# Splitting the segment recurrence into memory rows and other rows, and loading half the heads in the weight gradients, in a training-step kernel on one core

## The chip, the cores and the metric

One NeuronCore of a Trainium2 chip runs the whole program. The metric is device time in microseconds (us) of one execution. A run is "fast" when it lies within 1.5% of the fastest run of the same kernel. The kernel before takes 6604.74 us (median of 4 runs, 6594.03 to 6612.77).

The names used below: PE is the matmul engine, PEld its weight loads, DVE the vector engine, ACT the scalar engine, POOL the third elementwise engine, SP the engine that only issues transfers. PEclk is the share of PE's clock that was granted.

## The reference

The kernel computes the output and all gradients of a recurrent attention layer, gated by a feed-forward layer. What matters here is the attention:

```python
# S = 2048, Dm = 640, H = 32 heads of 128, M = 8 memory rows, segments of 32 rows
for s in range(64):
    h = concatenate([mem, x[32 * s : 32 * s + 32]])        # 40 rows
    q, k, v = h @ Wq, h @ Wk, h @ Wv                       # 32 heads each
    p = softmax(mask(q @ k.T * scale))                     # memory rows see all 40, the others causally
    o = (p @ v) @ Wo                                       # 40 rows of 640
    mem = o[:8]                                            # carried to the next segment
    outs.append(o[8:])                                     # not carried
# ... feed-forward, gate; then the backward pass through the same 64 segments,
#     and the gradients of Wq, Wk, Wv, Wo from the stored q, k, v, o
```

Only eight of the forty output rows are carried from one segment to the next. The other 32 are stored and used later.

## The kernel before

The forward recurrence treats the 40 rows as one block. Each segment builds v, then for three groups of heads (12, 12, 8) the projections, the scores, the softmax and the product with v, and at last the output projection `pso`. The next segment starts from the copy of `pso` into `hT`.

```python
for t in range(T):                                  # T = 64
    hT = hTs[t % 2]
    ...                                             # pv: values of the 8 memory rows, 40 matmuls of 512 columns
    def scores_softmax_group(h0, nh):
        for hh in range(nh):                        # psc: 40x40 scores, one matmul for each head
            nc.tensor.matmul(psc[:, hh, :], qT[:, hidx, :], kT[:, hidx, :], ...)
        nc.vector.tensor_tensor(smv, pscv, k.maskq[0:L, 0:nh, :], ALU.add)
        nc.vector.reduce_max(mx[:, 0:nh], smv, axis=AX.X)
        nc.vector.tensor_tensor(smv, smv, bc_last(mx[:, 0:nh], L), ALU.subtract)
        nc.scalar.activation(exv, smv, ACT.Exp, scale=k.scale)
        nc.vector.tensor_reduce(zs[:, 0:nh], exv, axis=AX.X, op=ALU.add)
        nc.vector.reciprocal(rz[:, 0:nh], zs[:, 0:nh])
        nc.gpsimd.tensor_tensor(Pseg[:, h0:h0 + nh, :], exv, bc_last(rz[:, 0:nh], L), ALU.mult)
    ...                                             # pt_ot_group: ppt, po and their copies to PTseg, oT
    for gi2, (h0, nh) in enumerate(hgroups):
        f1_group(h0, nh)                            # pj: projections, 320 matmuls of 40 columns in all
        scores_softmax_group(h0, nh)
        if gi2 >= 1:
            pt_ot_group(*hgroups[gi2 - 1])
    vt_all()
    pt_ot_group(*hgroups[ng - 1])
    for dc in range(DC):                            # pso: 160 matmuls of 40 columns
        for jc in range(H):
            nc.tensor.matmul(pso[:, dc, :], Wo[:, jc, dc * P:(dc + 1) * P], oT[:, jc, :], ...)
    nc.vector.tensor_copy(hTs[(t + 1) % 2][:, :, 0:M], pso[:, :, 0:M])     # the carried rows
    ...                                             # stores of q, k, v, o, p
```

The last stage builds token-major copies of q, k, v and o, 16 heads ("a half") at a time, from 64 stored tiles each:

```python
ft = srp.tile([P, H, L], BF16, name="fullx", tag="fullx", bufs=10)
k.dma(ft[:], XT[t].rearrange("p (h l) -> p h l", l=L))                     # all 32 heads, 320 KB
...
nc.vector.tensor_copy(xsrc[:, :, j, :], fulls[j][:, hs:hs + H2, M:L])      # 16 of them are used
```

One helper issues nearly all transfers.

```python
self.dma_engines = [nc.sync, nc.scalar]
def dma(self, out, in_, eng=None):
    if eng is None:
        eng = self.dma_engines[self._dma_i % len(self.dma_engines)]
        self._dma_i += 1
    return eng.dma_start(out, in_)
```

## Time and profile before

| | before |
|---|---|
| time, median of 4 runs | 6604.74 us |
| span of the profiled run | 6603.7 us |
| forward recurrence (first `pv` to first epilogue transpose) | 1886.5 us |
| backward recurrence (first `pgh` to first `w2acc`) | 2259.4 us |
| weight gradients of the attention (first `gacc` to last `oacc`) | 1098.4 us |

The profile page of the kernel before begins with busy times. It then shows the span in 40 equal slices of 165 us; each digit is a share in tenths (busy share for PE, granted clock for PEclk, busy share of the transfer engines for DMA).

```profile
PE 5397.4 (82%) x112777; PEld 4213.5 (64%) x112978; DVE 2551.8 (39%) x5102; ACT 1765.0 (27%) x3076; POOL 346.0 (5%) x782
...
PE   6868887777777766999999999999555877888878
...
PEclk9888777777777767999899998999757998999989
DMA  5363332222222255222222222222666855455552
```

Slices 4 to 14 are the forward recurrence: PE at 7 or 8, its clock at 7 or 8, transfers at 2 or 3. Nothing is full there. From the 35th slice on, the weight gradients show PE at 7 or 8 with the clock at 8 or 9 and transfers at 4 or 5 until the last slice: short stretches in which loads, not PE, set the pace. These are the two places at which the change aims.

### The profile page before, as it was taken

What the parts mean: (1) busy time and instruction counts of PE and PEld (TensorE: products, weight loads), DVE (VectorE), ACT (ScalarE), POOL (GpSimd) and SP (SyncE); (2) the same over time, 40 slices, a digit from 0 to 9 for tenths busy, and PEclk for the clock granted to TensorE, in tenths of its full rate; (3) what the DMA queues carried; (4) which work ended last, traced back from release to release, by engine and by line L of the source; (5) the groups of instructions that cost most, each with busy time, mean ns of one, the idle gap of its engine ahead of it and who ended that gap; (6) DMA issues with size and microseconds to landing.
All of it is one profiled execution on the core that took longest, in us unless ns stands there. A gap on an engine that the chain in (4) does not pass through costs nothing.

```text
span 6603.7 us, 244712 instructions
## 1 busy us (share of the span) xinstructions
PE 5397.4 (82%) x112777; PEld 4213.5 (64%) x112978; DVE 2551.8 (39%) x5102; ACT 1765.0 (27%) x3076; POOL 346.0 (5%) x782
## 2 busy tenths in 40 slices
PE   6868887777777766999999999999555877888878
PEld 3426777666766656888888888888422444444445
DVE  5424544444444443444434334433225622222222
ACT  3313333223223221222222222222113112232222
POOL 0000000000000000000000000000000001111110
PEclk9888777777777767999899998999757998999989
DMA  5363332222222255222222222222666855455552
GB/s 179 126 218 110 100 112 66 63 67 61 63 67 61 63 152 201 79 78 79 79 73 78 75 76 78 75 76 78 72 191 202 192 138 199 148 185 201 181 169 99
DMA packets 795893, 760.71 MB, mean 115 GB/s; under 512 B 444016, under 2 KB 625264, under 8 KB 790256
## 3 DMA queue, kind: packets, MB, share of 16 engines
q1 hardware_dynamic: 452638, 375.93, 19.5%
q10 hardware_dynamic: 338450, 348.15, 17.1%
q8 instruction: 883, 14.47, 0.9%
q0 software_dynamic: 3776, 20.97, 0.8%
q14 instruction: 146, 1.20, 0.1%
HBM read 453.95 MB, written 290.89 MB: 113 GB/s over the span
## 4 chain that ended last, share of the span: by engine, by line
PE 60%; DMA 15%; DVE 12%; issue 5%; ACT 4%; POOL 2%; ACTq 0%; another core or an unknown queue 0%; POOLq 0%; DVEq 0%; SPq 0%
PE pgh L806 12%; PE gacc L1160 5%; PE pso L579 5%; PE pj L518 4%; PE pgo L729 4%; PE oacc L1186 2%; PE pv L497 2%; POOL Pseg L541 2%; PE pgot L782 2%; PE pgxb L968 2%; DMA hb_tok<-HB 2%; PE ptokk L774 2%; PE pvx L471 2%; DMA fullx<-GQT 2%; PE wacc L1042 2%
## 5 line engine op out<-in xcount | busy, mean ns | idle before, releaser
L1160 PE MATMUL gacc<-gtok_all,h_all 128*128 128x512 bf16 x2322 | 554.3, 387 | 42.2 <-ACT gtok_all L94 10.8
L579 PE MATMUL pso<-oT,Wo 128*128 128x40 bf16 x10240 | 379.3, 197 | 74.0 <-ACT oT L94 73.9
L1160 PEld LDWEIGHTS <-h_all 128*128 128x128 bf16 x2400 | 236.0, 99 | 313.8 <-issue 73.6
L579 PEld LDWEIGHTS <-Wo 128*128 128x128 bf16 x10240 | 355.5, 107 | 45.9 <-issue 34.2
L806 PE MATMUL pgh<-gQT,WqT 128*128 128x40 bf16 x10240 | 348.8, 182 | 11.1 <-issue 7.0
L806 PE MATMUL pgh<-gKT,WkT 128*128 128x40 bf16 x10240 | 330.3, 181 | 22.8 <-DMA WkT<-WKT 14.0
L94 ACT COPY qtok<-ptokq 40x1024 bf16<-40x1024 bf16 x128 | 128.8, 1006 | 768.5 <-PE ptokq L774 759.8
L806 PE MATMUL pgh<-gVT,WvT 128*128 128x40 bf16 x10240 | 320.2, 181 | 10.2 <-issue 9.0
L518 PE MATMUL pj<-hT,Wq 128*128 128x40 bf16 x10240 | 322.3, 185 | 0.2
L806 PEld LDWEIGHTS <-WqT 128*128 128x128 bf16 x10240 | 303.6, 97 | 22.3 <-issue 9.0
L518 PEld LDWEIGHTS <-Wq 128*128 128x128 bf16 x10240 | 296.3, 100 | 33.6 <-issue 28.2
L806 PEld LDWEIGHTS <-WkT 128*128 128x128 bf16 x10240 | 294.0, 97 | 28.3 <-DMA WkT<-WKT 14.1
L518 PE MATMUL pj<-hT,Wk 128*128 128x40 bf16 x10240 | 309.9, 185 | 0.8 <-ACT oT L94 0.6
L811 DVE CAST goT<-pgh 128x40 bf16<-128x40 f32 x63 | 12.6, 199 | 767.0 <-PE pgh L806 767.0
L806 PEld LDWEIGHTS <-WvT 128*128 128x128 bf16 x10240 | 289.6, 96 | 13.9 <-issue 11.5
L729 PE MATMUL pgo<-goT,WoT 128*128 128x40 bf16 x10240 | 277.9, 180 | 25.0 <-DMA WoT<-WOT 15.2
L518 PEld LDWEIGHTS <-Wk 128*128 128x128 bf16 x10240 | 293.4, 100 | 1.1 <-issue 1.0
L729 PEld LDWEIGHTS <-WoT 128*128 128x128 bf16 x10240 | 268.1, 96 | 34.8 <-DMA WoT<-WOT 15.3
L541 POOL TENSOR_TENSOR Pseg<-ex,rz 40x480 bf16<-40x480 bf16 (+1 forms) x192 | 171.9, 895 | 2229.1 <-DVE rz L540 2210.7
L1129 PE MATMUL pt<-ident,xsrc 128*128 128x128 bf16 x2048 | 162.1, 237 | 115.5 <-DVE xsrc L1118 63.0
L1129 PEld LDWEIGHTS <-xsrc 128*128 128x128 bf16 x2048 | 141.5, 107 | 169.0 <-issue 80.8
L1121 POOL COPY msrc<-fullx 128x128 bf16<-128x128 bf16 x512 | 152.8, 324 | 1685.0 <-DMA fullx<-GQT 980.4
(228 smaller groups left out, 9116.8 us busy)
## 6 DMA issues: line engine op xcount, KB each, us to landing
fullx<-GQT SPq DMA_DIRECT2D x64, 320.0 KB
fullx<-GQT ACTq DMA_DIRECT2D x64, 320.0 KB
fullx<-GKT SPq DMA_DIRECT2D x64, 320.0 KB
fullx<-GKT ACTq DMA_DIRECT2D x64, 320.0 KB
fullx<-GVT SPq DMA_DIRECT2D x64, 320.0 KB
fullx<-GVT ACTq DMA_DIRECT2D x64, 320.0 KB
fullx<-OT SPq DMA_DIRECT2D x64, 320.0 KB
fullx<-OT ACTq DMA_DIRECT2D x64, 320.0 KB
```

The lines of the kernel that those rows point to most:

```text
L471: nc.tensor.matmul(pvx[:, :], xnTt[:, dc, :], Wv[:, dc, jn * 512:(jn + 1) * 512], start=(dc == 0), stop=(dc == DC - 1))
L497: nc.tensor.matmul(pv[32 * q:32 * q + M, :], hT[:, dc, 0:M], Wv[:, dc, jn * 512:(jn + 1) * 512], start=(dc == 0), stop=(dc == DC - 1), til ...
L518: nc.tensor.matmul(pj[:, hh, :], W_[:, dc, hidx * P:(hidx + 1) * P], hT[:, dc, :], start=(dc == 0), stop=(dc == DC - 1))
L541: nc.gpsimd.tensor_tensor(Pseg[:, h0:h0 + nh, :], exv, bc_last(rz[:, 0:nh], L), ALU.mult)
L579: nc.tensor.matmul(pso[:, dc, :], Wo[:, jc, dc * P:(dc + 1) * P], oT[:, jc, :], start=(jc == 0), stop=(jc == H - 1))
L729: nc.tensor.matmul(pj[:, hh, :], WoT[:, dc, hidx * P:(hidx + 1) * P], goT[:, dc, :], start=(dc == 0), stop=(dc == DC - 1))
L774: nc.tensor.transpose(ptk[:, hh, :], src[:, b8 + hh, :], k.ident[:, :])
L782: nc.tensor.transpose(ptk[:, hh, :], gOT[:, hs + b8 + hh, :], k.ident[:, :])
L806: nc.tensor.matmul(pso[:, dc, :], WT_[:, jc, dc * P:(dc + 1) * P], gX[:, jc, :], start=(i_acc == 0), stop=(i_acc == n_acc - 1))
L1121: nc.gpsimd.tensor_copy(msrc[:, mt2, :, r4, j * M:(j + 1) * M], fulls[j][:, hs:hs + H2, 0:M])
L1129: nc.tensor.transpose(pt8[0:nrow, hh, :], xsrc[:, b8 + hh, 0:nblk, :], k.ident[:])
L1160: nc.tensor.matmul(accs[dc][:, :], h_all[:, kt, dc * P:(dc + 1) * P], gtok[:, kt, jn * 512:(jn + 1) * 512], start=(kt == 0), stop=(kt == N ...
```

## The change

Its intent is twofold. First, the chain that is carried from segment to segment shall hold only what the eight memory rows need: 8 rows x 32 heads = 256 rows, packed into two blocks of 128. The other 32 rows of segment t are worked on one step later, beside the memory rows of segment t+1. Second, the last stage shall load only the 16 heads it uses, into 24 buffers instead of 10. The core of the diff:

```diff
+        def mem_attention(t, qT, kT, vtile):
+            for hidx in range(H):          # psT: scores of 8 rows, keys on the partitions
+                nc.tensor.matmul(psT[:, hidx, :], kT[:, hidx, :], qT[:, hidx, 0:M], start=True, stop=True)
+            nc.scalar.copy(sTm[:], psT[:])
+            for g in range(NGT):           # two transposes: 256 rows on the partitions
+                nc.tensor.transpose(ps2[:, g, :], sTm2[:, g * P:(g + 1) * P], k.ident[0:L, 0:L])
+            nc.vector.reduce_max(mx[:], ps2[:], axis=AX.X)
+            ...
+                nc.scalar.activation(Em[:, g, :], ps2[:, g, :], ACT.Exp, bias=nmx[:, g:g + 1], scale=k.scale,
+                                     accum_out=Zm[:, g:g + 1])
+            ...                            # rZm, Pm, back by two transposes to PTm
+                nc.tensor.matmul(pom[:, hidx, :], vtile[:, hidx * P:(hidx + 1) * P], PTm2[:, hidx * M:(hidx + 1) * M],
+                                 start=True, stop=True)
+            nc.scalar.copy(oTc[:, :, 0:M], pom[:, :, :])
+        def x_attention(tp, qT, kT, vtile):   # the other 32 rows, as before, of segment t-1
+            ...
-                ex = wk.tile([L, 12, L], BF16, name="ex", tag="ex")
+                ex = wk.tile([NXQ, 12, L], BF16, name="ex", tag="ex")     # the pool had 2 buffers, now 1
+            ...
+        for step in range(T + 1):
+            ...
+                mem_attention(t, qT, kT, vtile)
+            if tp >= 0:
+                x_attention(tp, qTs[tp % 2], kTs[tp % 2], vts[tp % 2])
+            emit_wT_units(units_per_step)     # 3 of the 136 weight transposes
-                    nc.tensor.matmul(pso[:, dc, :], Wo[:, jc, dc * P:(dc + 1) * P], oT[:, jc, :],
+                    nc.tensor.matmul(pso[:, dc, :], Wo[:, jc, dc * P:(dc + 1) * P], oTc[:, jc, :],
@@ backward @@
-            nc.vector.tensor_tensor(prod[:], gOT[:], oT_s[:], ALU.mult)
+            nc.vector.tensor_tensor(prod[:, :, 0:M], gOT[:, :, 0:M], oT_a[:, :, 0:M], ALU.mult)
+            nc.vector.tensor_tensor(prod[:, :, M:L], gOT[:, :, M:L], oT_b[:, :, M:L], ALU.mult)
@@ weight gradients @@
-                ft = srp.tile([P, H, L], BF16, name="fullx", tag="fullx", bufs=10)
-                k.dma(ft[:], XT[t].rearrange("p (h l) -> p h l", l=L))
+                    ft = srp.tile([P, H2, L], BF16, name="fullx", tag="fullx", bufs=24)
+                    k.dma(ft[:], XT[t].rearrange("p (h l) -> p h l", l=L)[:, hs:hs + H2, :])
```

Left out: the second buffers of q, k and v, the mask tables that are now built after the stage before, the shifted store of o (its memory columns go to row t, the others to row t+1), and the load of two such rows in the backward pass and in the last stage.

## The prediction

> **What bounds the kernel now.** I read three things in this order: busy time by stage, the chain of waits inside one forward step, and busy time in slices of the last stage.
>
> The stages are told apart by which tiles are written. The forward recurrence (64 segments, tile pso) runs from 533 to 2416 us, the backward recurrence (pgh) from 2520 to 4716, and the weight gradients of the attention (gacc, oacc) from 5490 to 6604. Busy time in those stretches (us of PE, PEld, DVE, ACT, POOL, then granted PE clock, DMA share, GB/s):
>
> ```profile
> 533.00:892.00 359.00, 303.96 (x8096) 265.20 (x8096) 176.71 (x358) 134.22 (x249) 31.74 (x35) 0.80 0.33 103
> 892.00:2416.00 1524.00, 1191.55 (x34017) 1068.85 (x34016) 694.95 (x1364) 466.61 (x897) 140.19 (x157) 0.76 0.23 68
> ...
> 2520.00:4716.00 2196.00, 2055.11 (x59121) 1904.80 (x59119) 863.77 (x1528) 584.46 (x1020) 13.62 (x63) 0.92 0.27 80
> ...
> 5490.00:6317.00 827.00, 684.52 (x4250) 361.53 (x4326) 202.24 (x460) 219.17 (x300) 122.77 (x410) 0.94 0.54 182
> ```
>
> The backward stage has PE busy 94% at clock 0.92: little to win there. The forward stage has PE busy 78% at clock 0.76, with DVE at 46% and ACT at 31%. No engine is full, so a chain of dependent steps bounds it. One step takes 28.94 us (pv from 1514.05 to 1542.99). Its chain, by time (start, length, what):
>
> ```profile
> 1514.05 2.33 PE pv L497 x40
> 1516.38 3.88 PE pj L518 x149
> 1520.27 0.47 PE psc L526 x12
> 1520.76 0.66 DVE smx L530
> ...
> 1522.81 0.61 ACT ex L536
> 1523.45 0.65 DVE zs L538
> ...
> 1525.05 0.99 POOL Pseg L541
> ...
> 1533.55 0.47 ACT ex L536
> ...
> 1537.94 0.43 ACT oT L94
> 1538.41 4.30 PE pso L579 x136
> 1542.74 0.21 DVE hT L583
> ```
>
> From 1520.76 to 1538.41 the chain walks through the softmaxes of three head groups on DVE, ACT and POOL; PE fills in projections where it can. The output projection pso waits for the last group, and the next segment waits for pso. In the weight gradient stage, half the heads take 134 us (one transpose block starts at 5647.77, the next at 5782.89, the next at 5917.00). The same columns for one such half, first its dense part, then its build part:
>
> ```profile
> 5710.21:5782.89 72.68, 68.17 (x307) 30.44 (x313) 9.02 (x16) 6.12 (x11) 5.18 (x18) 1.00 0.28 92
> 5782.89:5845.67 62.78, 43.61 (x402) 28.19 (x408) 24.03 (x61) 29.72 (x40) 14.05 (x46) 0.92 0.81 271
> ```
>
> In the build part the DMA share is 0.81, and the waits show what for:
>
> ```profile
> L1118 DVE COPY xsrc<-fullx 128x512 bf16<-128x512 bf16 x43 | 12.2, 313 | 31.1 <-DMA fullx<-GKT 31.0
> ```
>
> So the build is paced by loads: 64 tiles of 320 KB per half (20.5 MB), of which only half the heads are used.
>
> **What the Trainium skill says.** "TensorE: Matmul & The Clock Gate", Back-to-back issue gap: below 64 columns a matmul costs a floor of about 25 ns however narrow it is. The trace agrees: 32 pgh matmuls of 40 columns start 0.812 us apart (3504.66 to 3505.47), 25.4 ns each, and 40x40 ones in the backward step cost the same. So halving the columns of a matmul saves nothing, and each added matmul costs 25 ns. The same page, The HAM clock gate: the PE clock falls to half after an idle window. The trace shows granted 0.76 in the forward against 0.92 in the backward stage; 136 pso matmuls after a stall took 4.30 us, 31.5 ns each. "DMA: Bandwidth & Descriptors", Why small descriptors are slow: about 3 cycles per packet, which at 1280 against 2560 bytes would be some 3% (my estimate from its formula). So halving the run length should nearly halve the load time; no row of this trace shows it alone. "Perfetto Trace Analysis", Optimization Strategy: interleaving regimes with different bounds can help, which is what this change does.
>
> **The change, part by part.**
>
> (1) Forward pipelining. Only the 8 memory rows of segment t feed segment t+1. The change computes these 8 rows for all 32 heads by themselves (packed as 256 rows: two transposes, one softmax of 128x80), and does the other 32 rows one step later, as filler. Their three softmaxes leave the loop-carried chain. I worked the new step out along the new kernel's order of instructions.
>
> PE work: pj 320, pso 160, and five sets of 32 (psT, psc, ppt, po, pvt) plus pom 32 = 672 narrow matmuls, plus 4 transposes: 676 x 25.4 ns = 17.2 us. With pv 2.33 us that is 19.6 us (before: 608 x 25.4 ns + 2.33 = 17.8 us).
>
> The chain: end of pj to sTm = drain 0.2 + last kT copy 0.49 + psT 0.35 + sTm 0.4 (256 columns, between 0.33 for 200 and 0.43 for 320 on ACT) + hand-overs = 1.5. sTm to ps3: psc and ps2 ahead 1.0, then on DVE mmx 0.25, mx 0.65, nmx 0.2, smx 0.65 and subtract 0.65 that stand between in its order, rZm 0.2, vT 0.4, Pm 0.25, hand-overs 0.35: 4.4. Em and the small reductions have no row of their own; I take the fixed cost of the 40-column DVE copies (0.2). Then ps3 0.3 + PTm 0.4 + pom 1.0 + oTc 0.4 = 2.1; pso 160 x 25.4 ns + drain + hT = 4.5; one ppt block 0.3; pv + pj = 10.5. Sum 23.3 us, so PE would still stall 3.7 us. I add 0.5 for a clock not fully granted: 23.8.
>
> Weight transposes: before, they ran inside the first steps (tile wTpt, 542 to 892 us), which took 29.4 us instead of 28.9, so they were almost free. Now three units of 4 or 5 transposes stand in each of 46 steps, partly in a stall, partly inside pso; they share one PSUM buffer with pvt, which moves into the pv block. I charge 0.5 + 1.0 = 1.5 us: 25.3 for those.
>
> Forward: 46 x 25.3 + 18 x 23.8 + 9 (a 65th step for the last 32 rows) + 5 (tables now built after the VX stage) = 1606 us, against 1883. Gain 277.
>
> (2) Half loads in the weight gradients. Each load takes the 16 heads in use, 160 KB, and there are 24 buffers instead of 10. Before, 10 tiles and the 16 that sit in four xsrc tiles were ready when a build began: the first 112 transposes ran in 11.7 us. Now 40 of 64 are ready, and the other 24 are 3.9 MB, 14 us at 271 GB/s, behind a build that is bound by PE: 320 transposes x 55 ns + 85 gacc x 216 ns = 36 us, and I allow 42 for short waits on copies (ACT has some 30 us of work there). That replaces 62.8. Five steady halves gain 20 each, the first (5490 to 5648, nothing prefetched) 32, the two of OT 17 and 13, as their PE work is larger: 162, say 165.
>
> (3) Backward: one more 320 KB load per step, hidden (DMA share 0.27), and prod in two pieces, 0.83 us to some 0.9 on DVE, which psD waits for: 64 x 0.1 = 6, say 8 us lost.
>
> Sum: 6605 - 277 - 165 + 8 = 6171, say 6170 us.
>
> **The rivals.** First: the memory chain becomes the new wait. It has a dozen hand-overs between PE, DVE and ACT, each behind other work in a strict order. DVE stands at 13.3 us of 28.9 per step now and gets about 1.5 more, so queueing is likely though the engine isn't full. 2 us more per step would give 6300, still faster. Second: PE becomes the bound and the chain hides in it fully, 21 us per step with the clock at 0.9: 6170 - 64 x 3.5 = 5950. Against it speaks that pso can't start before pom and its copy, and nothing large is left to fill those stalls. Third: the loads of the last stage were hidden anyway, or short runs move no faster per packet, so nothing is gained: 6335. Against it: the 31 us wait of xsrc on fullx per half. Fourth: the build gets as short as PE work alone, 104 us per half: about 60 us better, 6110. A slower kernel would need the forward step to stay above 29 us and the last stage to gain nothing.
>
> **Range and chances.** The forward gain is the uncertain term (200 to 370), the last stage 110 to 220. Taken together 6060 to 6280 should hold it 8 times in 10. Faster by over 2% (below 6473) 0.97, within 2% 0.025, slower 0.005.
>
> **What would show it.** In the changed profile: the distance of hT copies should be near 23.8 late and 25.3 early in the forward stage; the chain there should name psT, sTm, Em, PTm, pom and pso, and no x softmax or POOL; the granted clock there should rise from 0.76 to 0.85 or more. A half of the weight gradients should take some 114 us, with the wait of xsrc on fullx near 5 us instead of 31. The backward step should stay at 34.3 to 34.5 us. I would be wrong if pso waits for x rows (ppt, po), if the stall before ps3 is over 3 us, or if builds still sit at a DMA share of 0.8.

## The result, and the profile after

All outputs are correct. Ratios here are the mean time of one kernel's fast runs over the mean of the other's in the same rounds, so not quite the ratio of the medians.

| | before | after |
|---|---|---|
| time, median | 6602.53 us (12 runs, 6594.03 to 6612.77) | 6266.26 us (8 runs, 6252.06 to 6289.4) |
| ratio, with 95% interval | 1 | 0.949 (0.9477 to 0.9503) |
| span of the profiled run | 6603.7 us | 6287.6 us |

The change gains 336 us of the predicted 434. The profiled run of the kernel after is the slowest of its eight, 23 us above the median, so the stages below sum to 316 us.

The same four lines of the page after the change:

```profile
PE 5450.7 (87%) x117284; PEld 4249.5 (68%) x117490; DVE 2564.7 (41%) x5429; ACT 1816.0 (29%) x3535; POOL 343.6 (5%) x782
...
PE   6859999999998849999999999999745788899989
...
PEclk9878888888888758989899898989855899999999
DMA  5353333333322282222222223222475774433441
```

In the forward slices (5 to 12, of 157 us) PE is now at 9, but its clock is still at 8. From the 35th slice on transfers are down from 4 or 5 to 3 or 4, and PE is at 8 or 9. Stage by stage, from the first instruction of each to that of the next (us):

| stage | before | after | change | predicted |
|---|---|---|---|---|
| up to the forward recurrence | 533.0 | 538.5 | +5.5 | +5 |
| forward recurrence | 1886.5 | 1663.2 | -223.3 | -282 |
| its epilogue | 119.5 | 121.6 | +2.1 | 0 |
| backward recurrence | 2259.4 | 2283.2 | +23.8 | +8 |
| feed-forward gradients, first part (`w2acc`, `pghb`) | 355.2 | 373.9 | +18.7 | 0 |
| feed-forward gradients, second part (`pgxb`) | 348.0 | 353.4 | +5.4 | 0 |
| attention weight gradients | 1098.4 | 949.6 | -148.8 | -165 |

(The prediction's forward gain of 277 includes the 5 us in the first row.)

Below are the stretches of the kernel after: the forward recurrence with weight transposes in its steps, and the later part without them. The columns are the stretch, its length, the busy times of PE, PEld, DVE, ACT and POOL with counts, the granted clock, the share of transfers, and GB/s.

```profile
538.50:1750.00 1211.50, 1150.71 (x34149) 1012.78 (x34150) 652.38 (x1479) 493.58 (x1189) 127.99 (x142) 0.83 0.31 90
1750.00:2197.00 447.00, 403.51 (x12449) 362.78 (x12446) 231.03 (x512) 166.01 (x415) 46.60 (x53) 0.81 0.24 71
```

In the first, PE is busy 95% (1150.71 of 1211.50), in the second 90%. The clock is 0.83 and 0.81, where the prediction asked for 0.85 or more. The distance of successive `hT` copies is 25.7 us in the first 45 intervals (25.3 predicted) and 25.85 in the later ones (23.8 predicted); in the kernel before it was 29.4 on average, 30.6 in the first eleven and 29.2 in the others.

**One early step.** The timeline of PE in the kernel after, with start, length, line, operation, tiles, shape and count:

```profile
1200.51 0.40 PE L617 MATMUL ps<-ident,Pm 128*40 128x128 bf16 x2
...
1201.98 1.01 PE L623 MATMUL pom<-PTm,vt 40*128 40x8 bf16 x32
...
1203.45 5.27 PE L699 MATMUL pso<-oTc,Wo 128*128 128x40 bf16 x160
...
1211.04 1.46 PE L582 MATMUL pv<-Wv,hT 128*8 128x512 bf16 x23
1212.44 1.69 PE L571 MATMUL pj<-hT,Wq 128*128 128x40 bf16 x60
```

The chain is the predicted one: `ps` (the transposes of Pm), `pom`, `pso`, then `pv` and `pj` of the next segment. Matmuls of the other 32 rows (`ppt`, `po`) stand before `pso` in PE's order, but it waits for none of their softmaxes and for no POOL operation: up to 1750 us PE is idle before `pso` in 3 steps only, 1.3 us in all, for the copy of `pom`. But `pso` takes 5.27 us, where 160 matmuls at 25.4 ns were counted as 4.06. The same stretch in slices of one microsecond (columns as above) shows why:

```profile
1196.00:1197.00 1.00, 1.00 (x35) 0.94 (x36) 0.28 (x1) 0.74 (x2) 0.00 (x0) 1.00 0.99 239
1197.00:1198.00 1.00, 1.00 (x36) 0.94 (x33) 1.00 (x3) 0.66 (x2) 0.00 (x0) 0.79 0.41 162
1198.00:1199.00 1.00, 0.98 (x28) 0.91 (x24) 1.00 (x4) 1.00 (x6) 0.00 (x0) 0.50 0.09 18
...
1206.00:1207.00 1.00, 1.00 (x36) 1.00 (x33) 0.00 (x0) 0.29 (x1) 0.68 (x1) 0.50 0.52 164
1207.00:1208.00 1.00, 1.00 (x38) 1.00 (x35) 0.67 (x2) 0.18 (x1) 0.00 (x0) 0.59 0.03 8
1208.00:1209.00 1.00, 1.00 (x41) 0.96 (x37) 0.20 (x1) 0.00 (x0) 0.71 (x1) 1.00 0.05 9
```

The clock falls to 0.50 at about 1197.6, in the stretch of narrow matmuls (`psc`, `po`, `ppt`), and it falls while PE has been busy without a pause (12.6 of the 12.6 us since 1185.0, as far as the profile shows, which models the ends of matmuls). It comes back at 1207.8. Nearly all of `pso` runs at half clock. In the timeline of a later step, 160 `pso` matmuls take 5.49 us, 34 ns each against the 25.4 ns of the prediction; from first start to last end `pso` takes 5.3 us on average in the early steps and 5.2 in the late ones.

"Narrow" needs care here: the projections `pj` have 40 columns too, over the full array, and through them the clock stays at 1.00. What follows them has only 8 columns, or uses only 32 or 40 rows or columns of the array, and some of it is transposes; these three were not told apart. In the early steps the clock fell 1.9 to 5.5 us after the last projection (median 3.7), and 66 of the 67 low stretches of the forward stage last 6.8 or 10.2 us. So a clock that falls before `pso` stays low into it.

**One late step.** The timeline of the kernel after around the end of `pso`, all engines:

```profile
2055.28 5.49 PE L699 MATMUL pso<-oTc,Wo 128*128 128x40 bf16 x160 [0.46 <-ACT oTc L625]
...
2058.17 0.60 ACT L648 ACTIVATE ex<-smx 32x480 bf16<-32x480 f32 x1 [2.45 <-POOL Px L653]
...
2060.92 0.47 ACT L648 ACTIVATE ex<-smx 32x320 bf16<-32x320 f32 x1 [2.15 <-POOL Px L653]
...
2061.42 0.47 DVE L650 TENSOR_REDUCE zs<-ex 32x8 f32<-32x320 bf16 x1 [1.66 <-ACT ex L648]
2061.82 0.18 DVE L703 CAST hT<-pso 128x40 bf16<-128x40 f32 x1
```

`pso` ends at 2060.77. The copy into `hT`, which the next segment needs, starts a microsecond later, because DVE runs in its program order and the sum `zs` of the other 32 rows stands before it. `zs` waits for `ex`, and `ex` waits for POOL to finish with the only buffer of `ex`. The waits of 1800 to 2160 us name it (waiting engine and tile, what it waited for, us in total, times, longest):

```profile
ACT ex L648 <- POOL Px L653: 56.5, 27, 2.5
```

**One half of the weight gradients**, its build part and its dense part, in the kernel after (columns of the stretches):

```profile
5691.08:5733.00 41.92, 39.17 (x405) 26.60 (x411) 24.99 (x66) 31.38 (x43) 11.94 (x41) 1.00 0.64 194
5733.00:5811.30 78.30, 73.50 (x357) 33.88 (x363) 10.48 (x19) 7.37 (x13) 6.31 (x24) 0.98 0.23 72
```

The build part fell from 62.8 to 41.9 us, as predicted (42), with PE busy 93%. The dense part is some 6 us longer than the 72.7 before.

**The feed-forward gradients**, which the change doesn't touch, got slower. First the waits in the kernel before (4798 to 5154 us), then those in the kernel after (4606 to 4980 us), and for each kernel the issues of one load of this stage:

```profile
ACT ghb L937 <- DVE dsl L945: 28.5, 37, 1.1
...
g5t<-GATET SPq DMA_DIRECT2D x52, 128.0 KB
```

```profile
ACT ghb L1062 <- DVE ggT L1074: 66.7, 24, 3.1
...
g5t<-GATET ACTq DMA_DIRECT2D x52, 128.0 KB
```

The load of `g5t` is issued by ACT now and was issued by SP before, although its code is the same: the new forward makes an odd number of calls of the alternating helper. ACT's copy `ghb` now waits for another operation of DVE and for longer.

From this reading came the theory to be tested: the mechanism is as predicted, and what is missing is (a) `pso` at half clock, (b) the `hT` copy behind a softmax that has only one buffer, (c) the swap of the issuing engines. The rivals were that the missing part is PE being simply full, that the depth of the buffers or the bytes were mis-sized in the last stage, or that the two halves of the change disturb each other.

### The profile page after: what moved, and what is told of

The parts are those of the page before. It is cut to its first block, busy times and chain, and to the rows that moved or that the text cites. A ratio compares the mean times of both kernels' runs of the same rounds, so it can differ in the third digit from the quotient of the medians.

```text
span 6287.6 us, 254570 instructions
## 1 busy us (share of the span) xinstructions
PE 5450.7 (87%) x117284; PEld 4249.5 (68%) x117490; DVE 2564.7 (41%) x5429; ACT 1816.0 (29%) x3535; POOL 343.6 (5%) x782
## 4 chain that ended last, share of the span: by engine, by line
PE 67%; DMA 14%; DVE 9%; ACT 5%; issue 3%; POOL 1%; ACTq 0%; another core or an unknown queue 0%; SPq 0%; DVEq 0%; POOLq 0%
PE pgh L931 13%; PE pj L571 8%; PE gacc L1296 6%; PE pgo L853 4%; PE pso L699 3%; PE pv L582 3%; PE oacc L1322 2%; DMA hb_tok<-HB 2%; PE pgxb L1093 2%; PE pgot L907 2%; PE pvx L527 2%; PE ptokk L899 2%; PE ptokq L899 2%; PE wacc L1167 1%; DVE u L873 1%
## 5 line engine op out<-in xcount | busy, mean ns | idle before, releaser
L699 PE MATMUL pso<-oTc,Wo 128*128 128x40 bf16 x10400 | 335.7, 195 | 8.2 <-ACT oTc L625 7.5
L699 PEld LDWEIGHTS <-Wo 128*128 128x128 bf16 x10400 | 335.9, 107 | 9.6 <-issue 6.4
L571 PE MATMUL pj<-hT,Wk 128*128 128x40 bf16 x10240 | 291.6, 180 | 3.2 <-issue 2.6
L571 PEld LDWEIGHTS <-Wq 128*128 128x128 bf16 x10240 | 273.4, 96 | 30.1 <-issue 30.0
L571 PE MATMUL pj<-hT,Wq 128*128 128x40 bf16 x10240 | 290.7, 180 | 1.1 <-ACT qT L94 0.5
L571 PEld LDWEIGHTS <-Wk 128*128 128x128 bf16 x10240 | 274.0, 96 | 4.7 <-issue 4.5
L653 POOL TENSOR_TENSOR Px<-ex,rz 32x480 bf16<-32x480 bf16 (+1 forms) x192 | 173.7, 905 | 1472.8 <-DVE rz L652 678.6
L92 DVE CAST kT<-pj 128x480 bf16<-128x480 f32 (+1 forms) x192 | 115.6, 602 | 301.2 <-PE pj L571 300.8
L92 DVE CAST gwo<-gacc 128x512 bf16<-128x512 f32 x72 | 49.7, 691 | 407.7 <-PE gacc L1296 289.7
L907 PE MATMUL pgot<-ident,gOT 128*40 128x128 bf16 x2048 | 205.5, 256 | 6.1 <-DVE ktok L92 4.5
```

The costliest lines, as they stand in the source:

```text
L92: return nc.vector.tensor_copy(out, in_)
L571: nc.tensor.matmul(pj[:, hh, :], W_[:, dc, hidx * P:(hidx + 1) * P], hT[:, dc, :], start=(dc == 0), stop=(dc == DC - 1))
L653: nc.gpsimd.tensor_tensor(Px[:, h0:h0 + nh, :], exv, bc_last(rz[:, 0:nh], L), ALU.mult)
L907: nc.tensor.transpose(ptk[:, hh, :], gOT[:, hs + b8 + hh, :], k.ident[:, :])
```

## The experiments

Eleven kernels ran, in three groups, each on one chip with runs of the kernel before beside it. All gave correct outputs. Ratios are to the kernel before of the same rounds.

| run | what it is | median us (runs) | ratio (95%) |
|---|---|---|---|
| wg_only | before + half loads | 6431.32 (4) | 0.9724 (0.9699 to 0.9748) |
| fwd_only | after - half loads | 6421.48 (4) | 0.971 (0.9691 to 0.973) |
| ex2 | after + second `ex` buffer | 6251.79 (4) | 0.9456 (0.9432 to 0.948) |
| fillpin | after + useless matmuls on parts of the array | 6461.59 (4) | 0.9768 (0.9748 to 0.9788) |
| parity | after + the old order of issuing engines | 6240.43 (5) | 0.945 (0.9435 to 0.9465) |
| half10 | after with 10 buffers | 6276.3 (4) | 0.9501 (0.9484 to 0.9519) |
| fillfull | after + useless matmuls on the whole array | 6349.19 (4) | 0.9617 (0.9599 to 0.9635) |
| best1 | ex2 and parity together | 6224.34 (4) | 0.9429 (0.9411 to 0.9446) |
| late14 | best1 + 14 useless wide matmuls, late steps only | 6256.11 (4) | 0.9472 (0.9448 to 0.9497) |
| late8 | best1 + 8 of them | 6247.52 (1) | one look |
| latethin | best1 + 94 useless narrow ones | 6287.39 (1) | one look |

### The two parts of the change alone: wg_only and fwd_only

```diff
--- before
+++ wg_only
-  ft = srp.tile([P, H, L], BF16, name="fullx", tag="fullx", bufs=10)
-  k.dma(ft[:], XT[t].rearrange("p (h l) -> p h l", l=L))
+  ft = srp.tile([P, H2, L], BF16, name="fullx", tag="fullx", bufs=24)
+  k.dma(ft[:], XT[t].rearrange("p (h l) -> p h l", l=L)[:, hs:hs + H2, :])
--- after
+++ fwd_only
   the reverse of this, for both loads of the new kernel
```

> Kernel before with part 2 alone (half loads and 24 buffers in the weight gradients). If the parts are independent, as both the prediction and the stage times of the changed kernel say (1098 to 950 us from the first gacc to the last oacc, 149 less), about 6453 us, ratio 0.977. The prediction's own size was 165, which would be 6437 us. Rival: the part only helps together with the new forward stage or the 34 us by which unchanged stages were longer in the changed kernel's profile come from here: then 6490 us or more.

> Changed kernel with the full loads and 10 buffers of before in the weight gradients, so part 1 and part 3 alone. From the stage times of the changed kernel: forward 223 us less, backward 21 us more, start 4 more: about 6402 us, ratio 0.970. If the 21 us of the backward stage are noise of one profile: 6385. The prediction's sizes (277 less, 8 more) would give 6334. The two gains of this and the run before should add up to the whole of 336 us.

wg_only gained 178 us (6609.4 to 6431.32); its weight gradient stage took 928.1 us instead of 1098.4, so 170 less, where 165 were predicted. Successive halves are 112.8 to 116.2 us apart, where 114 were predicted. This part of the prediction was right in size.

fwd_only gained 188 us, less than any of the three sizes of its expectation, which left out the feed-forward gradients. Its forward recurrence took 1661.4 us, as in the kernel after (1663.2), and its steps 25.7 us throughout. So the shortfall of the forward part is there without the other half of the change. Its feed-forward gradients took 372.6 and 356.1 us, as slow as in the kernel after, while those of wg_only stayed at 358.6 and 346.7: the slowdown there comes with the new forward.

The two gains sum to 366 us, and the full change gained 336. The weight gradient stage gained 170 alone and 149 with the new forward; so the two parts do disturb each other a little. The run "parity" says how.

### A second buffer: ex2

```diff
--- after
+++ ex2
-  ex = wk.tile([NXQ, 12, L], BF16, name="ex", tag="ex")
+  ex = wk.tile([NXQ, 12, L], BF16, name="ex", tag="ex", bufs=2)
   (to make room: the mask is kept once for each row, and read by a repeating access pattern)
```

> Changed kernel with two ex buffers (as before the change; the mask is read by a repeating access to make room). Theory: in the last 18 steps hT waits on DVE behind the last zs, which waits for ex, which waits until POOL has read the only ex buffer (the trace has hT 1.05 us after pso ended at 2060.77); with two buffers that wait goes and these steps get some 0.7 us shorter, the early ones, in which PE is 95% busy, not at all: 10 to 15 us in all, 6253 us. Rival: the chain through the memory softmax sets the late steps, and the extra buffer changes nothing: 6266 us.

The early steps hardly changed (25.71 to 25.59 us), the late ones fell from 25.85 to 25.01, the forward recurrence from 1663.2 to 1643.9, and the total from 6266 to 6252. In the waits of 1800 to 2160 us, `ex` on POOL, 56.5 us in the kernel after, no longer stands among the six largest. The intervals of the two ratios overlap at their ends (0.9432 to 0.948 and 0.9477 to 0.9503), so the total alone would not show it. The steps do: late ones take 25.70 to 25.88 us in the four kernels with one buffer and no fill (after, fwd_only, parity, half10), and 25.01 and 25.04 in the two with a second one (ex2, best1). In the late steps `hT` starts 0.88 us after the end of `pso` in the kernel after, and 0.04 us in ex2. So theory (b) holds and is worth 0.8 us of the 2.0 that the late steps are over the prediction. The early steps have nearly nothing to gain: `hT` waits 0.12 us there, and PE is busy 95% of the time.

### Useless matmuls against the falling clock: fillpin and fillfull

If the clock falls because few columns pass the array, then useless wide matmuls in that stretch should hold it. fillpin takes its data from the chain itself, and so uses only 40 rows or 40 columns of the array for each; fillfull uses all 128 x 128.

```diff
--- after
+++ fillpin
+  for _ in range(2):     # behind sTm, Em, Pm and PTm; 8 matmuls of 480 columns in each step
+      nc.tensor.matmul(dum[0:m, :], <sTm2 | Em | Pm | PTm2>, Wk_[0:r, 0, 0:480], start=True, stop=True)
--- after
+++ fillfull
+  for _ in range(2):     # behind the last kT copy (480 columns) and each copy into oTc (384, 384, 256)
+      nc.tensor.matmul(dum[:, 0:w], Wq[:, 0, 0:P], <kT | oTc>, start=True, stop=True)
```

> Changed kernel with 8 useless matmuls of 480 columns per step, each pair tied to sTm, Em, Pm or PTm so that it runs in the stretch of narrow matmuls before pso; results unchanged. Theory: the clock falls to 0.50 there because narrow matmuls count as little work though PE is busy, and pso then runs at 34 ns a matmul. If the wide ones hold the clock, pso takes 4.1 us instead of 5.3 to 5.5, the granted clock of the forward stage rises from 0.83 to above 0.9, and against 1.7 us of added work per step (8 x 0.2) the step stays near 25.6 or falls by up to 1 us: 6200 to 6280 us. Rival: the clock falls because of idle gaps of PE or for a reason outside these instructions: pso stays at 5.3 us or more and the time rises by 8 x 0.2 us x 64 = 100 us, to 6370.

> Changed kernel with 8 useless matmuls per step that use the full 128x128 array (256 to 480 columns, 1.25 us per step at full clock, 2.5 at half), spread over the narrow stretch by their inputs (kT and the three written parts of oTc); results unchanged. Theory (narrow matmuls count as too little work for the clock): with full-array work spread over the stretch the clock holds longer, pso takes 4.1 to 4.6 us instead of 5.3, the step is 25.5 to 26.5 us, time 6270 to 6330. Rival (the clock falls whatever stands there, as in the run with eight useless matmuls on parts of the array): pso 5.3 us, 2.5 us more per step, 6420 to 6440 us.

Both lost. fillpin cost 195 us over the kernel after, nearly twice what even its rival expected: the clock fell at 1211.8, one microsecond after the first useless pair began, and later pairs then ran at half clock (0.99 us a pair in the timeline), straight in the chain. Whether they failed to hold the clock because they came too late or because they use only part of the array was not told apart, so the run says little about the theory.

fillfull cost 83 us, between the two expectations. One-microsecond slices of its step at 1204 to 1227 us, around the fall:

```profile
1214.00:1215.00 1.00, 1.00 (x30) 0.87 (x30) 0.21 (x1) 0.28 (x2) 0.00 (x0) 1.00 0.85 311
1215.00:1216.00 1.00, 1.00 (x20) 0.59 (x16) 0.70 (x3) 1.00 (x5) 0.00 (x0) 0.93 0.02 3
1216.00:1217.00 1.00, 1.00 (x26) 0.90 (x26) 0.87 (x3) 0.67 (x4) 0.00 (x0) 0.50 0.00 0
```

The last projection of this step ends at 1212.2, so the clock held 3.6 us after it, no longer than in the kernel after (median 3.6 us over the early steps, against 3.7). It fell with PE at 1.00, and `pso` still took 0.96 + 4.36 us. In its late steps, though, the fall came 7.5 us after the last projection (median, against 3.8), the mean clock was 0.88 instead of 0.82 and a step 26.10 us instead of 25.85 in spite of the added work, some 1.3 us at the full clock (my estimate: 3008 columns at the 216 ns that 512 columns take in `gacc`). That called for a test in the late steps alone, where PE has idle time to give; the runs late14, late8 and latethin below.

### The order of issuing engines: parity

```diff
--- after
+++ parity
+    k._dma_i += 1                       # one step of the alternation, no transfer
     phase5_Bbwd_ln(k, out_1, out_7, out_8, out_9)
```

> Changed kernel with one count added to the alternation between the two DMA issuing queues (SP, ACT) before the stage after the backward recurrence, so that from there on every load and store sits on the queue that it had before the change (the gate loads g5t on SP, the gup stores on SP, and so on); nothing else differs. Theory: the stages whose code the change does not touch were 16 to 19 us longer (first w2acc to first pgxb) and 5 to 8 us longer (to first gacc) in all four kernels with the new forward stage and not in the two with the old one, because an odd number of DMA calls swapped all later queues; this run loses that, and part of the 20 us by which the weight gradients gain less (149 against 170 alone): 6230 to 6245 us. Rival: it is noise or the placement in DRAM: 6266 us.

parity took 6240 us, 26 less than the kernel after. The issues of its trace show the old engine again:

```profile
g5t<-GATET SPq DMA_DIRECT2D x52, 128.0 KB
```

Its feed-forward gradients took 360.6 and 344.3 us (before 355.2 and 348.0, after 373.9 and 353.4), and its weight gradients 930.7, as alone (928.1), not 949.6; halves are 112.3 to 114.9 us apart instead of 114.8 to 120.2. The intervals of the two ratios don't overlap (0.9435 to 0.9465 against 0.9477 to 0.9503). The wait of `ghb` for `ggT` is no longer among the ten largest. So theory (c) holds, and the loss that the two halves of the change inflict on each other, some 20 us in the last stage, is this swap as well. With full loads the last stage didn't care for the order (1097.8 us in fwd_only against 1098.4). Which single wait in the last stage carries it was not traced.

### Bytes or depth: half10

```diff
--- after
+++ half10
-  ... name="fullx", tag="fullx", bufs=24)
+  ... name="fullx", tag="fullx", bufs=10)      # both loads
```

> Changed kernel with 10 buffers of half size in the weight gradients instead of 24. Prediction's model: 26 of 64 tiles are ready when a build begins, the other 38 are 6.2 MB, 23 us at 271 GB/s, still less than a build of about 42 us, so halving the bytes does nearly all and the depth nothing: 6266 to 6275 us. Rival: the depth hides the loads behind the dense part: some 10 us per half lost, 6340 us.

10 buffers took 6276 us, 24 took 6266: the intervals of the ratios overlap (0.9484 to 0.9519 against 0.9477 to 0.9503). The copies that wait on the loads, in the last stage of the kernel after and of half10 (busy us, mean ns, then idle time before them and what ended it):

```profile
L1254 DVE COPY xsrc<-fullx 128x512 bf16<-128x512 bf16 x249 | 69.2, 312 | 53.3 <-DMA fullx<-GQT 20.4 <-DMA fullx<-GKT 17.4 <-DMA fullx<-GVT 13.1
```

```profile
L1254 DVE COPY xsrc<-fullx 128x512 bf16<-128x512 bf16 x249 | 72.2, 319 | 77.5 <-DMA fullx<-GQT 26.9 <-DMA fullx<-GKT 24.2 <-DMA fullx<-GVT 24.0
```

The tiles of o stand in rows of their own, with 13.9 and 22.2 us. In the kernel before, one row has all four kinds, with 242.5 us for 344 copies; the rows here leave out 9 copies before the first `gacc`. Halving the bytes takes away most of it; 14 more buffers take away another 32 us of idle DVE time, of which at most some 10 reach the end.

### Both repairs: best1

> Two ex buffers and the restored queues together. If both effects are real and independent: 6266 - 14 - 30 = 6215 to 6230 us, faster than the changed kernel. Rival: 6250 us, as with two ex buffers alone.

6224 us, within the expectation and the fastest kernel, 0.9429 of the kernel before. Its steps are 25.56 us early and 25.04 late, its later stages as in parity (362.3, 344.6, 931.9). The gains of ex2 (14) and parity (26) add up (42).

### The clock in the late steps: late14, late8, latethin

```diff
--- best1
+++ late14 (late8: 2, 2, 0)
+  if t >= 46:
+      2 x nc.tensor.matmul(dumA[:, 0:480], Wq[:, 0, 0:P], kT[:, 20:32, :], ...)         # behind the last kT copy
+      3 x nc.tensor.matmul(dum[:, 0:nh * 32], Wq[:, 0, 0:P], oTc[:, h0:h0 + nh, M:L], ...)  # in each group
+      3 x nc.tensor.matmul(dumB[0:80, 0:480], Pm, Wk_[:, 0, 0:480], ...)                # behind Pm
+++ latethin: the same places, 8 columns each, 16, 18 in each group, and 24
```

> The fastest kernel so far (second ex buffer, restored alternation: 6224 us, late steps 25.04 us), with 14 useless wide matmuls in each step without weight transposes (segment 46 on): 2 of 480 columns behind the last key projection, 3 in each group behind its copy into oTc, 3 of 480 columns (80 weight columns) behind Pm. They use some 2.6 us of PE at the full clock, of which up to 2.6 us of a late step's idle PE time can take up nearly all. Theory A (the half clock in the stretch of narrow matmuls is due to few columns passing the array, and costs 160 x 8.8 ns = 1.4 us in pso alone): the clock stays at 1.00 longer, most of pso runs at 25 ns, pso takes 4.1 to 4.6 us instead of 5.3 to 5.5, and a late step gets 0.5 to 1.2 us shorter, 23.9 to 24.5, the kernel 6205 to 6217. Rival B (the clock falls whatever is put in, or it doesn't matter): pso stays over 5.2 us and late steps get 0.5 to 2 us longer, 25.5 to 27, the kernel 6230 to 6260.

> As the run with 14, but with 8 (2 and 2 in each group, none behind Pm), as in the run that put 8 into every step, where late steps fell to the half clock only at the beginning of pso. Theory A: the clock falls at about the beginning of pso, pso 4.6 to 5.2 us, late steps 24.5 to 25.0. Rival B: late steps 25.3 to 26.

> Control: the same places, but matmuls of 8 columns, 16 + 3 x 18 + 24 = 94 of them, which keep PE as busy (94 x 25 ns = 2.4 us) and pass few columns. Theory A: the clock falls as early as without them, pso stays at 5.3 to 5.5 us, late steps 25.0 to 26.5. Rival C (what counts is PE being busy): the clock stays up as with the wide ones, pso 4.1 to 4.6 us.

The stretch of 1760 to 2160 us in best1, in late14 and in latethin, in this order (columns as before; the clock is the third number from the end):

```profile
1760.00:2160.00 400.00, 370.22 (x11500) 334.06 (x11499) 212.40 (x487) 154.16 (x387) 44.02 (x49) 0.81 0.26 74
```

```profile
1760.00:2160.00 400.00, 383.25 (x10937) 314.11 (x10934) 194.89 (x450) 144.72 (x358) 41.48 (x45) 0.91 0.25 70
```

```profile
1760.00:2160.00 400.00, 379.80 (x11365) 348.42 (x11362) 189.15 (x420) 135.73 (x337) 37.45 (x42) 0.77 0.23 66
```

late14 and latethin keep PE equally busy (383 and 380 us), but the wide matmuls raise the clock from 0.81 to 0.91 and the narrow ones lower it to 0.77. In latethin the clock fell 1.8 to 5.0 us after the last projection (median 3.3 over the late steps), as in best1 without any fill (1.7 to 4.5, median 3.4); in late14 it did not fall at all in 8 of 16 late steps, and in one step it held until 2066.3, 11 us after the last projection. So rival C, that being busy is enough, is refuted as far as the single run of latethin shows, and the clock follows something nearer to the columns that pass the array. In the slice before that fall at 2066.3 PE was busy only 0.35, so idle time may count as well; that was not tested. In one thing theory A missed: latethin's late steps took 28.7 us, not 25.0 to 26.5.

As a repair the fill failed. late14 took 6256 us where theory A expected 6205 to 6217, and its late steps 26.9 us on average. They alternate. PE's timeline has these two `pso` in a row:

```profile
1879.31 4.41 PE L712 MATMUL pso<-oTc,Wo 128*128 128x40 bf16 x160
...
1909.41 5.01 PE L712 MATMUL pso<-oTc,Wo 128*128 128x40 bf16 x160
```

The step from the one at 1855.17 to 1879.31 is 24.1 us, inside what theory A expected, with `pso` at 4.41. But best1's late steps alternate too, between 24.1 and 25.6 us on average, so its short steps are just as short: what `pso` gained, the fill took. The next, to 1909.41, is 30.1 us: there the fill itself ran at half clock (three 384-column matmuls in 1.14 us instead of 0.66), and transposes of v, which wait for DVE, now stood before `pso` in PE's order. So `pso` does get shorter where the fill held the clock (4.2 to 4.5 us in every second step instead of 4.8 to 5.5 in best1), but no step and no kernel got faster by it; what the half clock costs the whole is not shown by a run. late8 held the clock at 0.89 and `pso` at 5.0 us, as theory A expected, but its late steps took 25.9 us, as its rival did.

## Why the prediction was right or wrong

**Direction, range and main mechanism: right.** 6266 us lies in 6060 to 6280, faster by 5%. The x softmaxes and POOL left the loop-carried chain, and the listed signs are there: `psT`, `sTm`, `Em`, `PTm`, `pom` and `pso` in the chain, and the only wait of `pso` in the later steps is for the copy of `pom` (5.1 us in 14 steps). One listed sign failed: the clock of the forward stage came to 0.83 and 0.81, not 0.85 or more.

**Weight gradients: right, seen alone.** The step "replaces 62.8" by 42 measured 41.9. The sum of 165 measured 170 in wg_only. In the full change it came to 149, as the swap of issuing engines cost some 20; the sign "xsrc on fullx near 5 us instead of 31" for each half came out at 20.4, 17.4 and 13.1 us over two halves each, so 7 to 10.

**Early forward steps: nearly right, in part by luck.** 25.3 predicted, 25.7 measured, x 46 = 19 us of the miss. The 25.3 was a chain with PE stalled for some 4 us, plus 1.5 for the weight transposes. Instead PE is busy 95% there, which the prediction's second rival had named (PE becomes the bound), but with the clock at 0.83, not 0.9, so that 21 us a step were never near. The ground for the 1.5 was misread as well: the first steps of the kernel before took 30.6 us, not 29.4, which is the mean of all steps, so the transposes were not "almost free" there.

**Late forward steps: the mis-sized term.** 23.8 predicted, 25.85 measured, x 18 = 37 us. Two terms of the chain failed:
- "pso 160 x 25.4 ns" with "0.5 for a clock not fully granted". The prediction saw `pso` at 31.5 ns in the kernel before and took it for the result of a stall, which would go as PE fills up. PE did fill up and the clock fell nevertheless; from first start to last end `pso` took 5.2 us on average in the late steps (4.9 to 5.5) instead of 4.06 + 0.2 (the drain, the time of its last matmul), so 0.9 more instead of 0.5.
- "drain + hT" with no queueing on DVE. The `hT` copy stood behind `zs`, `ex` and POOL, because the smaller pool leaves one `ex` buffer. ex2 measures this at 0.8 us a step. The prediction's first rival had the kind ("each behind other work in a strict order") but not the place.

Together they make 1.2 to 1.3 of the missing 2.05 us. The trace of the late steps places the rest: from the end of `pj` to `sTm` 1.9 us (1.5 predicted), from there to the transposes of Pm 4.0 (4.4), from these to the copy of `pom` 2.6 (2.1), while `hT`, `pv` and `pj` with one block of transposes took the 11.0 that were predicted. These add 0.6 us; the last 0.1 or so is the one step at the end of the weight transposes (27.7 us), which the mean of 25.85 includes. What lengthens the two short stretches was not tested.

**Not foreseen: the swap of issuing engines.** parity measures 26 us. The prediction looked at bytes and queue depth of transfers and never counted the calls of the alternating helper.

**Backward: open.** +8 was predicted for `prod` in two pieces and a further load. fwd_only has this backward code and took 2259.2 us, as before (2259.4), and fillfull 2260.4. But the kernel after took 2283, parity 2281 and best1 2280, and the other six kernels with this code lie between 2268 and 2279. The instructions of fwd_only and of the kernel after are the same up to the last stage; over this stage the granted clock is 0.911 in the first and 0.885 in the second. Over all 13 profiles the stage takes 2258 to 2260 us where the clock is 0.898 or more, and 2268 to 2283 where it is 0.895 or less. So the difference goes with the clock of the single run and is no fixed cost of the changed lines; why the clock differs stays open.

## What to carry to other kernels

Split a recurrence by what is really carried: the eight memory rows' own softmax and a one-step delay of the rest took 3.5 us off each of 64 steps, though PE got 68 more matmuls in each. When you estimate a chain of many narrow matmuls, take the durations at the clock that this stretch is granted, and don't expect a fuller PE to raise it; and when buffers are cut to make room, ask which in-order engine stands behind the one that is left. A helper that alternates issuing engines couples far-apart stages: count its calls, or set the engine by hand for each stage.

## What the Trainium skill lacked or had wrong

- "TensorE: Matmul & The Clock Gate", section "The HAM clock gate", explains the half clock by idle windows and says that activity releases it. For ordinary matmuls it lacks that those of few columns, or on part of the array, count as little activity: with PE busy throughout (12.6 of 12.6 us before 1197.6), the clock fell to 0.50, in the early steps 1.9 to 5.5 us after the last projection; 94 added matmuls of 8 columns left it so (0.77 on average, one run), and 14 added wide ones of about the same busy time raised it to 0.91. Matmuls of 40 columns over the full array kept it at 1.00. The page's two states, half and full, agree with the slices here, 0.50 and 1.00; the floor of about 25 ns agrees with 25.4 ns at the full clock, and 40-column matmuls took 34 ns at the half clock.
- "DMA: Bandwidth & Descriptors", section "Issuing engines are not separate DMA queues", says that initiating on several engines saves only the sequencer's time, which is usually small. It lacks that which of two engines issues can matter: exchanging them for the stages after the backward recurrence cost 26 us (6240 to 6266) with the same transfers. Of the 49 us by which the two profiled runs differ, 22 lie in the feed-forward gradients and 19 in the attention weight gradients.
- No page that I found gives the time of the extra instruction by which an activation with an accumulator writes its sum; it took 0.20 us each here (128 of them, 25.1 us), beside 0.29 us for the 128x40 exponential itself.
